# Late query and value remainders of a block-sparse attention and MoE kernel: other rows, one operation, no clearing

## Chip, cores and metric

The kernel runs on one core of a Trainium2 chip. The metric is the device time of one execution in microseconds (us). Five engines work from queues of their own, each in order: TensorE (PE, with its weight loads PEld), VectorE (DVE), ScalarE (ACT), GpSimd (POOL) and SyncE (SP), whose queue issues all the DMA transfers here.

## What is computed

Attention over 4 batches, 8 heads, 768 positions, head size 64. Each query sees its neighbours within 16 positions and 24 blocks of 32 positions, each block by its element-wise maximum of keys and its mean of values. Then a layer norm and a two-matrix feed-forward layer (512 to 2048 to 512) with a residual.

```python
k_sum = k.reshape(B, H, nb, block, D).max(axis=3)
v_sum = v.reshape(B, H, nb, block, D).mean(axis=3)
scores_l = scale * np.matmul(q, k.transpose(0, 1, 3, 2))
mask_l = np.abs(pos[:, None] - pos[None, :]) < window
scores_s = scale * np.einsum('bhsd,bhnd->bhsn', q, k_sum) + np.log(block)
scores_all = np.concatenate([np.where(mask_l, scores_l, -1e9), scores_s], axis=-1)
a = softmax(scores_all)
x = np.matmul(a, np.concatenate([v, v_sum], axis=2))     # heads side by side: [B, S, 512]
xn = (x - mean(x)) / np.sqrt(var(x) + 1e-6) * g_ln
out = x + np.maximum(xn @ w_ch1, 0.0) @ w_ch2
```

## The kernel before

The work is cut into 24 query tiles of 128 positions, each in two halves of four heads: 48 half tiles t. The first 12 (batch 0) run in float32 ("early"). The other 36 ("late") run in pairs of float16 numbers: each float32 operand is scaled by a power of two and split into its rounded value ("high") and the remainder ("low"), so that float16 matmuls give nearly float32 sums. The feed-forward layer works on 12 groups of two query tiles, again with pairs; g1 makes hidden units (h, then hh and hl), g2 adds their products into accumulators (a).

Three steps of a late half tile matter here.

- `load_q` (L601) loads the query tile twice, on rows 0 to 63 and on rows 64 to 127. ACT writes the high part to all 128 rows of qhl, then DVE overwrites rows 64 to 127 with the remainder. The key tiles hold the same 64 rows twice as well, so that one matmul contracts both parts of the query.
- `load_v` (L630) loads 128 rows of values into part 0 of vst and the tail with the block means into part 1. Part 1 holds the same data on rows 0 to 63 and on rows 64 to 127: `pv` (L787) contracts it with the high part of the last probabilities on the upper copy and with their remainder on the lower one. ACT writes the high halves of the float16 tile v16 (in the profile: v), DVE the low halves in two operations: 128 rows of part 0, and 64 rows of part 1. The low half of part 1 on rows 64 to 127 stays as `go_late` (L451) left it, zero.
- `transp` (L685) splits the probabilities and sends them through a transposing DMA to pT, which `pv` multiplies with the value tile.

Other names: raw, wf and wp are weights as loaded, decoded and split; kmax and vsum are maxima and sums of blocks; xn and xs are the normalised tile and its transposed pair; ksg, kh and kl are the keys; tx is the PE transposition of xn in the first groups; hl is the remainder of a hidden unit; spare is a filler.

No order is written by hand. A planner (class `Plan`) records every operation with an estimated cost and its dependences, and in 32 rounds of list scheduling looks for an order of all five queues; the best round is issued (`issue`, L352; hence all instructions carry line L373). Where PE would wait over 800 ns while the first weights are prepared, the planner puts fillers, small transpositions (spare, L370), in front of the wait. Two of its cost rules touch the change: a DVE operation costs its width over 0.96 plus a fixed part, and 119 ns are added where its first operand begins on row 64.

```python
fixed = {"tensor_tensor_reduce": 78, "reciprocal": 90}.get(op, 70) + 61 * pointers
fixed += 119 * (self.box(ins[0])[1] == D)
return n / (1.92 if op == "tensor_scalar" and not psum else 0.96) + fixed, 0.0
```

Of the kernel before, what the change touches and what calls it, by code (L numbers as in the profile page):

```python
# [15 lines left out]
F16 = mybir.dt.float16  # L16
U32 = mybir.dt.uint32
AF = mybir.ActivationFunctionType
ALU = mybir.AluOpType
AX = mybir.AxisListType  # L20

B, H, S, D = 4, 8, 768, 64
DM, DFF = 512, 2048
P = 128
# [38 lines left out]
    qs=("qs", "qw0"),  # L63
# [314 lines left out]
def body(ctx: ExitStack, tc, qt, qa, qe, kt, ks, va, vb, vs, g_ln, w1, w2, blocks, out):  # L378
# [5 lines left out]
    def work(tag, name, shape, dt=F32, bufs=1):  # L384
        return pl.tile(wp, shape, dt, tag, name, bufs)
# [17 lines left out]
    nc = pl  # L403
# [5 lines left out]
    late = {}  # L409
# [40 lines left out]
    @pl.step  # L450
    def go_late():  # L451
        late["p"] = prob[0], work("k0_0", "p3", [P, 4, NE])
        for x in late["p"]:
            nc.gpsimd.memset(x[:, :, NC:], 0.0)
        for i in range(2):
            t = late["v", i] = work(f"v16_{i}", f"v16_{i}", [P, 2, 4, 2, D], F16)
            nc.gpsimd.memset(t[:], 0.0)

    turn = {}

# [6 lines left out]
    def stg(tag, shape, dt=F32):  # L467
        stg_n[0] += 1
        if tag == "bst1":
            tag = ("bst", "qs")[stg_n[0] % 2]  # L470
        elif tag in ("bst", "qs"):
            tag = home(tag)
        return work(tag, f"{tag}{stg_n[0]}", shape, dt, 1 + (tag == "xn"))
# [126 lines left out]
    @pl.step  # L600
    def load_q(t):  # L601

        T, hh = divmod(t, 2)
        qs = stg('qs', [P, 4, P])
        for half in range(2):
            nc.sync.dma_start(qs[D * half : D * half + D], qt[T, hh])
        qhl = work(f"qhl{t % 2}", f"qhl{t}", [P, 4, P], F16)
        sc = bt["s", T // NT][:, 1:2]
        nc.scalar.activation(qhl[:], qs[:], AF.Copy, scale=sc)
        nc.vector.scalar_tensor_tensor(qhl[D:], qs[D:], sc[D:], qhl[D:], ALU.mult, ALU.subtract)  # L610
        st[t, "q"] = qhl

    @pl.step
# [15 lines left out]
    @pl.step  # L629
    def load_v(t):  # L630
        T, hh = divmod(t, 2)
        vt = vst[hh]
        nc.sync.dma_start(vt[:, 0], va[T, hh])
        for half in range(2):
            nc.sync.dma_start(vt[64 * half : 64 * half + 32, 1], vb[T, hh])
        w = late["v", hh]
        sv = bt["s", T // NT][:, 0:1]
        nc.scalar.activation(w[:, :, :, 0, :], vt[:], AF.Copy, scale=sv)
        for rows, i in ((P, 0), (D, 1)):
            nc.vector.scalar_tensor_tensor(  # L640
                w[:rows, i, :, 1, :], vt[:rows, i], sv[:rows], w[:rows, i, :, 0, :], ALU.mult, ALU.subtract
            )

    @pl.step
    def qk(t):
# [346 lines left out]
    def attend(t):  # L992
        if t < NEARLY:
            early_k(t)
            early_qk(t)
            for pr in range(2):
                softmax(t, pr)
            for pr in range(2):
                early_transp(t, pr)
                early_pv(t, pr)  # L1000
        else:
            load_q(t)
            for pr in range(2):
                load_k(t, pr)
            qk(t)
            for pr in range(2):
                softmax(t, pr)
            load_v(t)
            transp(t)
            pv(t)  # L1010
        if t % 2 and t < 8:
            norm(t // 2)
        if t == 3:
            spare()
# [29 lines left out]
    for t in range(NEARLY):  # L1044
        if t % 2 == 0:
            fetch_tail(t // 2)
        attend(t)
    go_late()

    for m in range(16):  # L1050
# [16 lines left out]
    for t in range(8, 2 * TT + 1):  # L1067
# [7 lines left out]
        b, i = divmod(t, 2 * NT)  # L1075
# [66 lines left out]
```

## Time and profile before

| | before |
|---|---|
| median of 3 runs | 633.12 us (632.31 to 633.8) |
| profiled execution, its own time | 633.28 us |
| its span, first to last instruction | 631.5 us |
| mean granted TensorE clock | 0.994 |
| DMA | 93.15 MB, mean 148 GB/s |

The span is what the trace covers; the execution's own time is 1.8 us longer. "Busy" of an engine is the time in which it has an instruction; PE's ends are modelled, so its pieces overlap slightly. In a timeline row the columns are start (us), duration (us), engine, line, operation and names (out<-in), shapes, count, and in brackets the idle time just before with what ended it. In a row of windows each engine has its busy time with the number of instructions; the last three columns are the granted clock, the DMA share and GB/s.

### The profile page before, as it was taken

What the parts mean: (1) busy time and instruction counts of PE and PEld (TensorE: products, weight loads), DVE (VectorE), ACT (ScalarE), POOL (GpSimd) and SP (SyncE); (2) the same over time, 40 slices, a digit from 0 to 9 for tenths busy, and PEclk for the clock granted to TensorE, in tenths of its full rate; (3) what the DMA queues carried; (4) which work ended last, traced back from release to release, by engine and by line L of the source; (5) the groups of instructions that cost most, each with busy time, mean ns of one, the idle gap of its engine ahead of it and who ended that gap; (6) DMA issues with size and microseconds to landing.
All of it is one profiled execution on the core that took longest, in us unless ns stands there. A gap on an engine that the chain in (4) does not pass through costs nothing.

```text
span 631.5 us, 13489 instructions
## 1 busy us (share of the span) xinstructions
PE 611.5 (97%) x4656; PEld 435.3 (69%) x4656; DVE 445.3 (71%) x1190; ACT 390.9 (62%) x1036; POOL 202.7 (32%) x413
## 2 busy tenths in 40 slices
PE   8988999999999999999999999999999999999997
PEld 5777766675676777667667677667766766666665
DVE  4799998999979999767956866866756844421212
ACT  4888898779988868768856674763763742110100
POOL 5221320023546536543533352533523512100000
PEclk9979999999999999999999999999999999999999
DMA  8980577626998888797855545556736513110000
GB/s 257 383 294 15 174 240 235 197 78 180 240 236 213 210 175 186 167 226 202 199 122 126 135 121 126 141 133 139 154 102 125 117 46 58 27 50 1 18 18 33
DMA packets 124997, 93.15 MB, mean 148 GB/s; under 512 B 84864, under 2 KB 107392, under 8 KB 124928
## 3 DMA queue, kind: packets, MB, share of 16 engines
q1 hardware_dynamic: 124928, 92.29, 56.1%
q8 instruction: 36, 0.59, 0.4%
q14 instruction: 33, 0.27, 0.1%
HBM read 66.27 MB, written 6.29 MB: 115 GB/s over the span
## 4 chain that ended last, share of the span: by engine, by line
PE 55%; DVE 18%; DMA 13%; ACT 4%; issue 4%; SPq 2%; POOL 2%; ACTq 0%; POOLq 0%; DVEq 0%
PE a L373 27%; PE h L373 24%; DMA ksg<-in_kt 4%; DMA raw<-in_w 3%; DMA qs<-in_qa 2%; DVE wf L373 2%; SPq L373 2%; PE o L373 2%; PE s L373 2%; DVE p L373 2%; DVE hl L373 2%; DMA bst<-in_vs 2%; DVE wp L373 2%; DVE raw L373 1%; DVE x L373 1%
## 5 line engine op out<-in xcount | busy, mean ns | idle before, releaser
L373 PE MATMUL h<-xs,wp 128*128 128x256 f16 x2304 | 272.7, 273 | 3.5 <-DVE hl L373 1.7
L373 PEld LDWEIGHTS <-wp 128*128 128x128 f16 x2304 | 223.6, 98 | 45.2 <-DVE hl L373 2.5
L373 PE MATMUL a<-wp,hh 128*128 128x512 f16 (+1 forms) x768 | 226.5, 377 | 0.0
L373 PE MATMUL a<-wp,hl 128*128 128x512 f16 x384 | 144.7, 377 | 0.0
L373 ACT ACTIVATE hh<-h 128x512 f16<-128x512 f32 x96 | 56.6, 590 | 132.1 <-PE h L373 104.3
L373 DVE SCALAR_TENSOR_TENSOR hl<-h,hh 128x512 f16<-128x512 f32 x96 | 65.6, 684 | 87.9 <-ACT hh L373 87.6
L373 PEld LDWEIGHTS <-hh 128*128 128x128 f16 x784 | 75.9, 98 | 63.2 <-issue 0.4
L373 ACT ACTIVATE p<-p,mn,sv 128x184 f32<-128x184 f32 x144 | 76.1, 530 | 19.1 <-POOL mn L373 17.9
L373 POOL TENSOR_TENSOR p<-p,p 128x512 f16<-128x512 f32 x72 | 69.4, 971 | 29.0 <-ACT p L373 26.3
L373 PEld LDWEIGHTS <-hl 128*128 128x128 f16 x392 | 38.3, 98 | 44.6
L373 DVE CUSTOM_DVE_ANT_0 p<-s,mask 128x184 f32<-128x184 f32 x144 | 43.3, 341 | 26.1 <-PE s L373 25.9
L373 ACT ACTIVATE kh<-ksg,sv 128x368 f16<-128x368 f32 x72 | 42.5, 593 | 19.2 <-POOL ksg L373 19.1
L373 POOL TENSOR_SCALAR mn<-mn,sv 128x2 f32<-128x2 f32 x72 | 31.7, 441 | 66.8 <-DVE mn L373 66.6
L373 DVE SCALAR_TENSOR_TENSOR x<-a,wsc,x 128x512 f32<-128x512 f32 (+1 forms) x48 | 35.3, 738 | 21.6 <-PE a L373 21.4
L373 DVE SCALAR_TENSOR_TENSOR kl<-ksg,sv,kh 128x368 f16<-128x368 f32 x72 | 46.1, 666 | 1.5 <-ACT kh L373 1.5
L373 POOL TENSOR_TENSOR x<-x,rc 128x256 f32<-128x256 f32 x36 | 24.9, 692 | 67.7 <-DVE x L373 63.7
L373 POOL COPY ksg<-ksum 128x48 f32<-128x48 f32 x72 | 21.5, 302 | 53.4 <-DMA ksg<-in_kt 44.0
L373 DVE SCALAR_TENSOR_TENSOR v<-vst,sv,v 128x256 f16<-128x256 f32 x72 | 38.1, 552 | 0.1
L373 ACT CAST p<-p 128x512 f16<-128x512 f32 x72 | 33.9, 504 | 0.3
L373 DVE TENSOR_REDUCE x<-o 128x256 f32<-128x512 f32 x36 | 24.5, 683 | 8.1 <-PE o L373 8.0
L373 PEld LDWEIGHTS <-pT 128*128 128x128 f16 x432 | 23.7, 98 | 7.3 <-DMA pT<-p 2.8
L373 PEld LDWEIGHTS <-qhl 128*128 128x128 f16 x288 | 24.0, 98 | 5.0
(128 smaller groups left out, 795.3 us busy)
## 6 DMA issues: line engine op xcount, KB each, us to landing
raw<-in_w SPq DMA_DIRECT2D x32, 512.0 KB
ksg<-in_kt SPq DMA_DIRECT2D x72, 184.0 KB
out_x<-x SPq DMA_DIRECT2D x23, 256.0 KB
qw<-in_qt SPq DMA_DIRECT2D x36, 128.0 KB
vst<-in_va SPq DMA_DIRECT2D x36, 128.0 KB
qs<-in_qt SPq DMA_DIRECT2D x36, 128.0 KB
vst<-in_vb SPq DMA_DIRECT2D x84, 32.0 KB
bst<-in_ks SPq DMA_DIRECT2D x12, 192.0 KB
```

The costliest lines, as they stand in the source:

```text
L373: getattr(getattr(nc, self.ops[i].engine), op)(*a, **k)
```

## The change

The query remainder goes to rows 0 to 63 instead of 64 to 127; since the key rows are there twice, the sum over both halves is the same. The value remainder is written by one DVE operation over both parts and all 128 rows. The low half of part 1 on rows 64 to 127 is then no longer zero but the remainder, which adds the product of both remainders to the result. As every element is now written, the two clearings of the value tiles on POOL go.

```diff
@@ go_late
         for i in range(2):
-            t = late["v", i] = work(f"v16_{i}", f"v16_{i}", [P, 2, 4, 2, D], F16)
-            nc.gpsimd.memset(t[:], 0.0)
+            late["v", i] = work(f"v16_{i}", f"v16_{i}", [P, 2, 4, 2, D], F16)
@@ load_q
         nc.scalar.activation(qhl[:], qs[:], AF.Copy, scale=sc)
-        nc.vector.scalar_tensor_tensor(qhl[D:], qs[D:], sc[D:], qhl[D:], ALU.mult, ALU.subtract)
+        nc.vector.scalar_tensor_tensor(qhl[:D], qs[:D], sc[:D], qhl[:D], ALU.mult, ALU.subtract)
@@ load_v
         nc.scalar.activation(w[:, :, :, 0, :], vt[:], AF.Copy, scale=sv)
-        for rows, i in ((P, 0), (D, 1)):
-            nc.vector.scalar_tensor_tensor(
-                w[:rows, i, :, 1, :], vt[:rows, i], sv[:rows], w[:rows, i, :, 0, :], ALU.mult, ALU.subtract
-            )
+        parts = [w[:, :, :, n, :].rearrange("p i j d -> p (i j) d") for n in range(2)]
+        nc.vector.scalar_tensor_tensor(
+            parts[1], vt.rearrange("p i j d -> p (i j) d"), sv, parts[0], ALU.mult, ALU.subtract
+        )
```

By the planner's rules the query operation gets cheaper by the 119 ns, and with the changed costs it finds another order for every queue. Three places follow; a minus marks a row of before only, a plus one of the change only.

On PE, around the preparation of the first weights, between the hidden unit h_306 and the hidden unit h_328 (wps is the sum that scales a weight block):

```order
 L373 MATMUL h_306<-xs_138,wp_300 128x256
-L370 MATMUL spare<-ident 128x128 x2
+L370 MATMUL spare<-ident 128x128 x3
 L373 MATMUL wps_0_317<-wacc,ones 128x8
+L370 MATMUL spare<-ident 128x128 x16
 L373 MATMUL tx_219<-ident,xn_218 128x128 x4
-L370 MATMUL spare<-ident 128x128 x11
+L370 MATMUL spare<-ident 128x128 x9
 L373 LDWEIGHTS wp_286
 L373 MATMUL h_328<-xs_192,wp_286 128x256
```

The 13 fillers of this gap become 28; with two other gaps (8 to 11 and 17 to 23) there are 69 fillers in place of 45.

On DVE, at the same time, the rows from the eviction of the transposed tile (xs_192), which h_328 reads, to the second half of the weight conversion wp_318 (wsc are the scales of a weight block, kmax block maxima). Before:

```order
L373 TENSOR_REDUCE kmax_408<-qs_413 128x12
L373 TENSOR_TENSOR xs_192<-tx_219,xs_192 128x512
L373 TENSOR_SCALAR wsc<-wsc 128x1
L373 TENSOR_SCALAR wf_344<-raw_301 128x512
L373 TENSOR_SCALAR wsc<-wsc 128x1
L373 TENSOR_SCALAR wf_345<-raw_302 128x512
L373 TENSOR_SCALAR wsc<-wsc 128x2
L373 SCALAR_TENSOR_TENSOR wf_344<-raw_301,wf_344 128x512
L373 TENSOR_REDUCE kmax_408<-bst_414 128x12
L373 SCALAR_TENSOR_TENSOR wp_318<-raw_273,wsc,wp_318 128x512
L373 SCALAR_TENSOR_TENSOR wp_318<-raw_274,wsc,wp_318 128x512
```

Now:

```order
L373 TENSOR_SCALAR wsc<-wsc 128x1
L373 TENSOR_SCALAR wf_344<-raw_301 128x512
L373 TENSOR_SCALAR wsc<-wsc 128x1
L373 TENSOR_SCALAR wf_345<-raw_302 128x512
L373 TENSOR_SCALAR wsc<-wsc 128x2
L373 SCALAR_TENSOR_TENSOR wf_344<-raw_301,wf_344 128x512
L373 TENSOR_TENSOR xs_192<-tx_219,xs_192 128x512
L373 SCALAR_TENSOR_TENSOR wp_318<-raw_273,wsc,wp_318 128x512
L373 TENSOR_REDUCE kmax_408<-qs_413 128x12
L373 TENSOR_REDUCE kmax_408<-bst_414 128x12
L373 SCALAR_TENSOR_TENSOR wp_318<-raw_274,wsc,wp_318 128x512
```

The eviction now stands behind six scaling and decoding operations that followed it, and ahead of one block maximum that preceded it; at the last row of each piece the sets ahead are equal.

On DVE, where the first late value tiles (v_0, v_1) are split. Before:

```order
L373 SCALAR_TENSOR_TENSOR v_0_263<-vst_77,sv_437,v_0_263 64x4x64
L373 SCALAR_TENSOR_TENSOR x_177<-a_4_0_406,wsc,x_177 128x512
L373 SCALAR_TENSOR_TENSOR x_123<-a_4_0_404,wsc,x_123 128x512
L373 SCALAR_TENSOR_TENSOR qhl_535<-qw_534,sv_437,qhl_535 64x512
L373 TENSOR_SCALAR rc_493<-sum_489,sv_437 128x4
L373 SCALAR_TENSOR_TENSOR v_1_264<-vst_78,sv_437,v_1_264 128x4x64
L373 SCALAR_TENSOR_TENSOR v_1_264<-vst_78,sv_437,v_1_264 64x4x64
```

Now:

```order
L373 SCALAR_TENSOR_TENSOR qhl_518<-qs_517,sv_437,qhl_518 64x512
L373 SCALAR_TENSOR_TENSOR v_1_264<-vst_78,sv_437,v_1_264 128x8x64
L373 TENSOR_REDUCE kmax_705<-qw_715 128x12
L373 SCALAR_TENSOR_TENSOR x_177<-a_4_0_406,wsc,x_177 128x512
L373 TENSOR_SCALAR rc_493<-sum_489,sv_437 128x4
L373 RECIPROCAL rc_493<-rc_493 128x4
L373 ISA p_262,mn_505<-s_0_503,mask_477 128x184
```

The value pair of v_1 has become one operation of 8 times 64 elements on 128 rows; the query operation keeps its shape, 64 rows of 512.

On POOL the two clearings, which stood on either side of the scaling of the block sums (vsum) at the start of the late stage, are gone.

## The prediction

> **What bounds the kernel now.** I read the page's first two parts, then busy times by stage, then TensorE's gaps one by one, then the chain of waits.
>
> ```profile
> PE 611.5 (97%) x4656; PEld 435.3 (69%) x4656; DVE 445.3 (71%) x1190; ACT 390.9 (62%) x1036; POOL 202.7 (32%) x413
> ...
> DVE  4799998999979999767956866866756844421212
> ```
>
> TensorE (PE) is busy for 97% of the span, so the ceiling of any edit elsewhere is small. VectorE (DVE) shows 71%, but its digits are 9 through most of the first 24 slices (380 us) and then fall away: the average mixes two regimes. The view by stages separates them (us, then busy us of PE, its weight loads, DVE, ACT, POOL):
>
> ```profile
> 50.00:75.00 25.00, 21.99 (x187) 18.95 (x186) 24.88 (x67) 21.27 (x64) 4.64 (x9) 1.00 0.24 76
> 100.00:125.00 25.00, 22.67 (x167) 16.27 (x168) 21.23 (x59) 21.26 (x64) 2.05 (x5) 1.00 0.62 201
> 143.00:280.00 137.00, 132.40 (x1076) 95.07 (x1075) 121.41 (x328) 112.56 (x296) 68.78 (x128) 1.00 0.84 202
> 300.00:600.00 300.00, 300.00 (x2287) 207.32 (x2286) 179.30 (x462) 144.72 (x346) 91.31 (x163) 1.00 0.45 102
> ```
>
> From 300 to 600 us PE never idles: what DVE saves there is worth nothing. From 143 to 280 us, where the late query tiles begin, PE idles 4.6 of 137 us while DVE is 89% busy. From 50 to 75 us DVE is full (24.88 of 25) and PE has 3 us of idle, besides fillers. So the span is PE's fixed work plus its gaps, and all gaps worth having lie before 280 us. PE's timeline lists them; the figure in brackets is the idle time and what ended it:
>
> ```profile
> 100.37 0.55 PE L373 MATMUL pp<-ident,p 128*128 128x128 f32 x3 [0.51 <-ACT p L373]
> ...
> 124.94 0.33 PE L373 MATMUL pp<-ident,p 128*128 128x128 f32 x1 [0.19 <-ACT p L373]
> ...
> 146.64 1.48 PE L373 MATMUL h<-xs,wp 128*128 128x256 f16 x12 [0.71 <-DMA xs<-x]
> ...
> 265.74 0.74 PE L373 MATMUL o<-v,pT 128*128 128x128 f16 x12 [1.27 <-DMA pT<-p]
> 279.08 1.49 PE L373 MATMUL h<-xs,wp 128*128 128x256 f16 x12 [1.53 <-DVE hl L373]
> ```
>
> The first two rows are the first and the last of five gaps between 100 and 125 us, 2.4 us in all; the others are three of six between 143 and 280 us, 4.6 us in all. None follows the last row until the work runs out.
>
> **The query remainder (36 operations).** Its width and row count stay; only the first row moves from 64 to 0. Durations alone say that this is worth nothing:
>
> ```profile
> L373 DVE SCALAR_TENSOR_TENSOR qhl<-qs,sv,qhl x18: 750/752/1104, 144.3 to 489.5; 64x512 f16<-64x512 f32 x18
> L373 DVE SCALAR_TENSOR_TENSOR wp<-raw,wsc,wp x31: 715/743/753, 44.0 to 153.8; 128x512 f16<-128x512 f32 x31
> ```
>
> The same operation of the same width from row 0 has a median of 743 ns against 752. But DVE operations overlap, and what counts is the distance from start to start:
>
> ```profile
> 59.36 2.74 DVE L373 SCALAR_TENSOR_TENSOR wp<-raw,wsc,wp 128x512 f16<-128x512 f32 x4
> 62.02 0.16 DVE L373 TENSOR_SCALAR rc<-sum 128x4 f32<-128x4 f32 x1
> ...
> 215.88 0.88 DVE L373 SCALAR_TENSOR_TENSOR v<-vst,sv,v 128x256 f16<-128x256 f32 x2
> 216.79 0.75 DVE L373 SCALAR_TENSOR_TENSOR qhl<-qw,sv,qhl 64x512 f16<-64x512 f32 x1
> 217.57 0.69 DVE L373 BATCH_NORM_STATS2 s<-x 128x6 f32<-128x512 f32 x1
> ```
>
> Four row-0 operations take 62.02 - 59.36 = 2.66 us, 0.665 each, and the next starts 0.08 us before the last ends. The query operation does not overlap: the value pair ends at 216.76 and it starts at 216.79; it ends at 217.54 and the next starts at 217.57. With the usual overlap it could have started at 216.68, so it occupies 217.57 - 216.68 = 0.89 us, and from row 0 it should occupy 0.665: **0.22 us less each**. The bounds are 0.01 (the medians) and 0.22; I take 0.22, because a 64-row operation from row 0, the second of the value pair, does overlap.
>
> [...]
>
> **The value remainder (72 operations become 36).**
>
> ```profile
> L373 DVE SCALAR_TENSOR_TENSOR v<-vst,sv,v 64x256 f16<-64x256 f32 x36 | 20.6, 572 | 0.0
> L373 DVE SCALAR_TENSOR_TENSOR v<-vst,sv,v 128x256 f16<-128x256 f32 x36 | 19.2, 533 | 0.0
> ...
> 225.51 0.79 DVE v L373 x2
> ```
>
> The last row is from the chain: the pair occupies 0.79 us. One 512-wide operation should occupy 0.665: **0.125 us less per tile**. The added rows 64 to 127 cost nothing, since the two forms of equal width differ by less than their spread (the 64-row form has the larger mean). The means, 0.55 us, lie above the 0.44 us of an undisturbed one, because some wait for POOL. Between "the wait per operation stays" and "per element stays" this is worth 0.1 us per tile or nothing; I take nothing.
>
> [...]
>
> **What of it reaches the end.** DVE saves 36 x 0.22 + 36 x 0.125 = 12.4 us in all. Before 280 us there are 16 query operations and 14 value pairs: 3.5 + 1.75 = 5.3 us. The chain says how much of them was waited for:
>
> ```profile
> 144.30 1.10 DVE qhl L373
> ...
> 221.43 0.76 DVE qhl L373
> ...
> 155.99 0.15 DVE v L373
> ...
> 242.35 0.87 DVE v L373 x2
> ```
>
> These are the first and last of five query pieces (4.2 us) and of ten value pieces (4.5 us) on the chain before 280 us. Five times 0.22 is 1.1 us, and 0.125 / 0.79 = 16% of 4.5 is 0.7 us: **1.8 us off the chain**. Bounds: nothing (another wait, such as the transposition DMA of the 1.27 us gap, ends equally late) and 4.6 us (every PE gap after 143 us closes). I take 1.8.
>
> **The dropped clearing.**
>
> ```profile
> L373 POOL MEMSET v<- 128x1024 f16 x2 | 1.9, 952 | 13.4 <-ACT wf L373 12.8 <-PE o L373 0.7
> L373 ACT ACTIVATE v<-vst,sv x36: 705/710/722, 150.3 to 532.2; 128x512 f16<-128x512 f32 x36
> ```
>
> The two clearings run at 127.8 and 129.8 us, POOL idles 13.4 us ahead of them, and the first reader of a value tile starts at 150.3 us. Twenty microseconds of other work cover them: 0 of at most 1.9 us. If the cover were gone, it would be the scaling of the block sums between them that gains.
>
> **The new order.** The planner's costs changed, so every queue is reordered from about 45 us on, before any edited instruction runs. Two places matter. First, TensorE gets 69 fillers instead of 45. Second, the eviction of the transposed tile that hidden unit h_328 waits for (xs_192) stands behind six more operations and one reduction fewer:
>
> ```profile
> 70.59 0.54 DVE L373 TENSOR_REDUCE kmax<-qs 128x12 f32<-128x384 f32 x1
> 71.05 0.68 DVE L373 TENSOR_TENSOR xs<-tx,xs 128x512 f16<-128x512 f32 x1
> 71.64 0.14 DVE L373 TENSOR_SCALAR wsc<-wsc 128x1 uint32<-128x1 uint32 x1
> ...
> 73.22 0.55 DVE L373 TENSOR_REDUCE kmax<-bst 128x12 f32<-128x384 f32 x1
> ```
>
> What stood between 71.64 and 73.22 (six operations, 1.58 us) is now ahead, the reduction (71.05 - 70.59 = 0.46 us) behind: PE starts that group **1.1 us later**. Its gap is filled anyway:
>
> ```profile
> 69.84 1.36 PE L370 MATMUL spare<-ident 128*128 128x128 f32 x11
> ...
> 71.78 5.29 PE L373 MATMUL h<-xs,wp 128*128 128x256 f16 x47 [0.47 <-DVE wsc L373]
> ```
>
> Eleven fillers take 1.36 us, of which the last one's modelled end is some 0.27: 0.109 us each, so 24 more are 2.6 us. By the weight conversion two microseconds on (wp_318), DVE has done the same set of operations in both orders, so DVE itself is not late; only PE is, by 1.1 us, and the 2.4 us of gaps between 100 and 125 us end with DVE, ACT and DMA events that PE's lateness leaves where they are. I cost it at 0; bounds 0 and +2.6 us.
>
> Sum against the profiled execution (633.28 us: a span of 631.5 and 1.8 around it): 633.28 - 1.8 = 631.5. That execution lies 0.16 us above the median shown, so I say **631.4 us**.
>
> **The rivals.**
> - Relief hidden: two of the three late gaps quoted end with a DMA, and the loads on SP's queue stay. A shorter DVE then only waits longer, and reordered queues open as many small gaps as they close: 633.1, within 1.2 either way. Against: DVE is 89% busy there.
> - More than the chain shows: the orders also let all gaps after 143 us close: 633.1 - 4.6 = 628.5. Against: each gap has another releaser.
> - Slower: the later start at 71 us and the 24 fillers are not recovered. Place: the gap ahead of h_328; price: up to 2.6 us; it decides if the five gaps from 100 to 125 us fail to shrink by as much as PE starts later. 633.1 + 2.6 = 635.7. For it: more fillers stand exactly where the planner leaves PE waiting.
> - The query operation does not get shorter, held for another reason than its first row: only the value term is left, 633.1 - 0.7 = 632.4.
>
> **How the numbers follow.** Chances: forecast 0.36 (630.2 to 632.6), hidden 0.28, more 0.11, slower 0.20, not shorter 0.05. A measurement of this kernel can tell about 0.2%, 1.3 us, from no change, so faster is below 631.8 and slower above 634.4. Three quarters of the forecast (0.27), all of "more" and a little of "hidden" (0.06) are faster: 0.44. Nearly all of the slower case and a little of hidden (0.03) are slower: 0.22. The rest, 0.34, is same. The range leaves out the lower half of "more" and the end of the slower case: 629.0 to 635.7.
>
> **What would show it.** Right: the query operation's start-to-start distance is 0.66 to 0.68 us and overlaps its neighbours; 36 value operations of about 0.74 us; DVE busy near 432; PE's gaps after 143 us sum to some 2.8 us, those from 100 to 125 us to about 1.3; the bulk of h_328 starts near 72.9. Wrong: a distance still near 0.8; gaps after 143 us of 4 us or more; PE gaps that reappear after 300 us; or the gap sum before 125 us grows by the fillers' 2.6 us.

## The result and the profile after

| | before | after |
|---|---|---|
| median of 19 runs each, beside each other | 633.60 us (632.22 to 637.13) | 637.85 us (634.62 to 640.60) |
| ratio, with its 95% interval | | 1.0059 [1.0041, 1.0077] |
| mean granted clock, mean over the runs that list it | 0.994 (17 runs of the next comparison) | 0.990 |

The change is slower, outside the forecast range (629.0 to 635.7). A second comparison of the unaltered change, told below, gave 1.0047 [1.0023, 1.0071]. The profiled execution of after is its fastest (634.62 us, span 632.8), so it shows the change at its best; a more usual execution comes further down.

The page's first part, after:

```profile
PE 612.6 (97%) x4680; PEld 437.4 (69%) x4680; DVE 433.6 (69%) x1154; ACT 392.3 (62%) x1036; POOL 207.2 (33%) x411
```

DVE's busy time fell by 11.7 us (445.3 to 433.6), almost the 12.4 us of the sum. The two edited operations, DVE's timeline of after (start, duration, names):

```profile
267.77 0.59 DVE L373 SCALAR_TENSOR_TENSOR kl<-ksg,sv,kh 128x368 f16<-128x368 f32 x1
268.28 0.74 DVE L373 SCALAR_TENSOR_TENSOR qhl<-qw,sv,qhl 64x512 f16<-64x512 f32 x1
268.94 0.73 DVE L373 SCALAR_TENSOR_TENSOR x<-a,wsc,x 128x512 f32<-128x512 f32 x1
...
272.56 0.72 DVE L373 SCALAR_TENSOR_TENSOR v<-vst,sv,v 128x512 f16<-128x512 f32 x1
273.22 0.67 DVE L373 SCALAR_TENSOR_TENSOR hl<-h,hh 128x512 f16<-128x512 f32 x1
```

From row 0 the query operation begins 0.08 us before its predecessor ends (268.36 against 268.28) and takes 268.94 - 268.28 = 0.66 us to the next start; the value operation takes 273.22 - 272.56 = 0.66. Both are the forecast 0.665 us. So these operations do what was said; the loss must come from elsewhere. Windows of after, with the columns as in the prediction:

```profile
100.00:125.00 25.00, 22.77 (x171) 16.82 (x170) 24.09 (x68) 21.25 (x65) 2.58 (x5) 1.00 0.79 254
...
143.00:280.00 137.00, 136.87 (x1115) 99.25 (x1113) 120.74 (x326) 116.01 (x305) 73.81 (x132) 1.00 0.89 211
280.00:300.00 20.00, 17.38 (x142) 12.09 (x141) 10.93 (x24) 15.11 (x42) 5.84 (x10) 1.00 0.75 188
```

From 143 to 280 us TensorE now idles 0.13 us in place of 4.6: more relief than forecast. But from 280 to 300 us it idles 2.6 us, in one piece, where before shows no idle time:

```profile
280.00:300.00 20.00, 20.00 (x163) 14.15 (x161) 14.21 (x38) 15.71 (x43) 7.62 (x14) 1.00 0.78 212
```

TensorE's timeline of after there, and SyncE's queue of DMA issues (SPq) just before:

```profile
288.79 1.47 PE L373 MATMUL h<-xs,wp 128*128 128x256 f16 x12 [2.62 <-DMA xs<-x]
```

```profile
283.37 0.34 SPq L373 DMA_DIRECT2D qw<-in_vs  x1
283.81 1.40 SPq L373 DMA_DIRECT2D qs<-in_qt  x2
285.31 1.28 SPq L373 DMA_TRANSPOSE xs<-x  x1
```

TensorE waits for the transposed tile xs, the first operand of a new group. DVE has finished that tile at 283.06; its transposing DMA is issued at 285.31, behind a load of value blocks (in_vs) for the next batch's sums and two loads of queries.

**A usual execution.** A second and a third profile were taken of the unaltered change. The second (633.33 us) is again the fastest of its runs; the third (638.48 us, span 636.7) is near the median and shows what the first two do not. Two of its windows, and TensorE's longer gaps in them:

```profile
100.00:125.00 25.00, 22.92 (x160) 16.29 (x159) 20.52 (x54) 18.82 (x57) 2.43 (x5) 0.93 0.73 224
...
280.00:300.00 20.00, 17.71 (x118) 11.68 (x116) 11.88 (x30) 15.36 (x42) 5.96 (x12) 0.91 0.82 218
```

```profile
105.89 0.38 PE L373 MATMUL wps<-wacc,ones 128*128 128x4 f32 x2 [1.18 <-ACT wf L373]
106.87 0.49 PE L373 MATMUL o<-vst,pT 128*128 128x128 f32 x2 [0.59 <-ACT pT L373]
...
291.06 2.20 PE L373 MATMUL h<-xs,wp 128*128 128x256 f16 x12 [2.29 <-DVE kl L373]
```

The gap at 288 to 291 us is there again. The view names DVE's kl as what ended it here, not the transposition; DVE came late to kl because a block sum just before it had waited for its load:

```profile
289.14 0.68 DVE L373 TENSOR_REDUCE vsum<-qw 96x16 f32<-96x512 f32 x1 [2.09 <-DMA qw<-in_vs]
```

Behind the gap the granted clock is 0.91 over the 20 us: the 12 matmuls after it take 2.20 us where they took 1.47 in the first profile. The same happened at 106 us (0.93 over 25 us). By estimate these two drops cost 25 x 0.07 + 20 x 0.09 = 3.5 us. In the comparison with 17 runs of before and 12 of the change beside each other, span times (1 - clock), averaged over the runs, is 3.9 us for before and 6.0 for after. By this estimate, **2.1 of the 3.1 us between the mean spans are clock.** It counts every stretch with a lower clock, the start too, where TensorE may have been waiting anyway.

How far TensorE has come with its useful work, each matmul of the trace counted by its columns at the distance of an undisturbed stream (0.107 us for 256 float16 columns) and fillers left out, in us of work; up to 1 us can be matmuls missing from a trace:

| | by 143 us | by 280 us | by 300 us |
|---|---|---|---|
| before | 122.1 | 251.3 | 271.2 |
| after, first two profiles | 119.6, 119.8 | 253.6, 254.2 | 270.8, 271.6 |
| after, usual execution | 118.2 | 250.8 | 266.8 |

The changed kernel is 2.3 to 3.9 us behind at 143 us, more than makes it up by 280 us in the first two profiles, and loses that again within the next 20 us. So the gap by itself does not explain the loss: with it, these two executions end within 1.3 us of before's profile (spans of 632.8 and 631.6 against 631.5). The third is 5.2 us longer; by 280 us it is 0.5 us behind, and from there to 300 us it does 16.0 us of work where before does 19.9.

### The profile page after: what moved, and what is told of

It is laid out like the page before. It is cut to its first block, busy times and chain, and to the rows that moved or that the text cites. A ratio compares the mean times of both kernels' runs of the same rounds, so it can differ in the third digit from the quotient of the medians.

```text
span 632.8 us, 13472 instructions
## 1 busy us (share of the span) xinstructions
PE 612.6 (97%) x4680; PEld 437.4 (69%) x4680; DVE 433.6 (69%) x1154; ACT 392.3 (62%) x1036; POOL 207.2 (33%) x411
## 4 chain that ended last, share of the span: by engine, by line
PE 69%; DVE 9%; DMA 9%; ACT 6%; issue 3%; SPq 2%; POOL 1%; ACTq 0%; DVEq 0%; POOLq 0%
PE a L373 31%; PE h L373 29%; PE s L373 3%; PE o L373 3%; ACT p L373 2%; DVE wf L373 2%; SPq L373 2%; DVE raw L373 2%; DMA qs<-in_qa 1%; PE v L373 1%; DMA ksg<-in_kt 1%; DMA qw<-in_qa 1%; DMA vw<-in_va 1%; DVE hl L373 1%; DMA bst<-in_ks 1%
## 5 line engine op out<-in xcount | busy, mean ns | idle before, releaser
L373 PE MATMUL h<-xs,wp 128*128 128x256 f16 x2304 | 271.6, 273 | 3.1 <-DMA xs<-x 2.6
L373 POOL TENSOR_SCALAR mn<-mn,sv 128x2 f32<-128x2 f32 x72 | 33.7, 470 | 55.3 <-DVE mn L373 54.8
L373 POOL TENSOR_TENSOR x<-x,rc 128x256 f32<-128x256 f32 x36 | 29.3, 815 | 66.3 <-DVE x L373 64.9
L373 DVE SCALAR_TENSOR_TENSOR kl<-ksg,sv,kh 128x368 f16<-128x368 f32 x72 | 44.3, 641 | 2.0 <-ACT kh L373 1.0
L373 DVE SCALAR_TENSOR_TENSOR v<-vst,sv,v 128x512 f16<-128x512 f32 x36 | 28.8, 801 | 2.3 <-ACT v L373 2.3
L373 ACT ACTIVATION_READ_ACCUMULATOR p<-p,mn,sv 128x1 f32 x144 | 27.4, 190 | 0.0
```

The lines of the kernel that those rows point to most:

```text
L373: getattr(getattr(nc, self.ops[i].engine), op)(*a, **k)
```

## Experiments

Every kernel was run beside before on the same chip; in the five comparisons the median of before was 633.7 to 634.3 us. The theories' names are those of the quoted expectations.

### Order or operations

The first kernel plans with before's operations and then issues the new ones in their places.

```diff
             nc.gpsimd.memset(t[:], 0.0)
+            pl.ops[-1].calls = []
...
+        pl.ops[-1].calls = [("scalar_tensor_tensor", (qhl[:D], qs[:D], sc[:D], qhl[:D], ALU.mult, ALU.subtract), {})]
...
+            pl.ops[-1].calls = []
+            if i == 0:
+                pl.ops[-1].calls = [("scalar_tensor_tensor", whole, {})]
```

> The changed operations in the order of before (the planner is shown the old operations, and the new ones are issued in their places; the second value operation and the clearings are left out). Theory ORDER (the loss of 4 us is the new order's): 0 to 2 us faster than before, since the order is the old one and DVE saves some 12 us of which 1.8 are on the chain. Rival OPERATIONS (one longer value operation holds POOL, or makes something late): slower than before by 2 us or more. Rival CLOCK (the loss is a lower granted clock that follows the early order): as ORDER for the time, with a clock as in before.

Measured: 642.25 us, ratio 1.0117 [1.0086, 1.0149], the slowest of the first four. Its DVE and PE timelines:

```profile
281.98 0.75 DVE L373 SCALAR_TENSOR_TENSOR v<-vst,sv,v 128x512 f16<-128x512 f32 x1 [5.47 <-DMA vst<-in_vb]
```

```profile
286.50 2.74 PE L373 MATMUL h<-xs,wp 128*128 128x256 f16 x12 [5.50 <-DVE hl L373]
```

The merged value operation waits 5.47 us for a load of tail rows, with h behind it. This shows a dependence that the prediction overlooked. Before, DVE read only rows 0 to 63 of part 1. So the load of rows 64 to 95 for the next tile but one, which uses the same buffer, needed to wait for ACT alone, and in the order of before 20 of these loads stand ahead of the place where the merged operation was put. It reads those rows now, and so waited for that load (and took its remainder there from that later tile). The kernel does not answer whether the order or the operations cost the time; a later one repairs it.

The second kernel is the opposite: the plan of the change, with before's operations issued (clearings beside the scaling of the block sums).

> The operations of before (query remainder on rows 64 to 127, two value operations, clearings) in the order of the change. ORDER: slower than before by 4 us or more, and slower than the change by 0 to 2 us. OPERATIONS: as before, within 1.5 us.

Measured: 639.66 us, 1.0089 [1.0065, 1.0113]; the unaltered change beside it:

> The change, unaltered, for another profile of it beside the others. All theories: 4 us above before. ORDER expects the difference in the gaps of TensorE before 150 us; CLOCK expects it in stretches with a clock below 1.00 before 60 us, with equal gaps.

636.46 us, 1.0047 [1.0023, 1.0071]. The operations of before alone, put into the new order, lose 5.9 us (639.66 against 633.75): **the order has a price of its own.** In that same order the new operations are 3.2 us faster than the old ones, so in the order planned for them they look like a gain, though the intervals just overlap; that order with them is still slower than before. The profile with the old operations has only 1.43 us of idle near 290 us, with a clock of 1.00, and is 2.4 us behind before by 280 us already: the long gap is not the only way in which this order loses.

### Fewer fillers

43 fillers in place of 69, at the same places.

```diff
+        keep, group, seen = (6, 8, 17, 2, 0, 9), -1, 0
...
+                if seen > keep[group]:
+                    continue
```

> The change with 43 fillers in place of 69 (per gap 8, 17, 2, 0, 9 in place of 11, 23, 3, 16, 9), nothing else altered. If the added fillers push TensorE's work back (the slower rival of the prediction): 1 to 2.6 us faster than the change. If they only fill waits: as the change within 1 us. CLOCK: as the change or slower, since a TensorE that idles longer is granted less.

Measured: 640.27 us, 1.0102 [1.0078, 1.0127], slower than with all 69. Its windows:

```profile
50.00:75.00 25.00, 20.90 (x169) 18.37 (x168) 23.17 (x66) 19.46 (x60) 2.85 (x7) 0.91 0.22 67
100.00:125.00 25.00, 23.23 (x156) 16.32 (x155) 23.02 (x65) 21.45 (x66) 4.27 (x8) 0.93 0.74 250
280.00:300.00 20.00, 16.20 (x100) 10.21 (x98) 11.83 (x32) 13.11 (x36) 5.84 (x14) 0.85 0.88 193
```

TensorE does not get on sooner without them, it idles, and the clock falls to 0.91 from 50 to 75 us, where the other profiles with that early order and its 69 fillers had 1.00 (in after with TensorE busy for 23.04 us of the 25). The added fillers are not the price that the slower rival took them for.

### Each edit alone, with an order of its own

> Only the query remainder moves to rows 0 to 63; the value remainder keeps two operations and the clearings stay; the planner makes its own order for it. Theory DRAW (what decides is which waits the new order happens to leave after 143 us, not which operation changed): the time lies anywhere from 632 to 641 us and follows from this run's own gaps and clock: 628 to 630 us of span times clock, plus its gaps over 0.5 us beyond those of before. Theory MERGE (the merged value operation is at fault): 632 to 633.5 us, as before or a little faster. Theory QUERY (the query operation on rows 0 to 63 is at fault): 636 to 638 us.

> Only the value remainder becomes one operation and loses its clearings; the query remainder stays on rows 64 to 127; the planner makes its own order for it. Theory DRAW: anywhere from 632 to 641 us, and the gaps and the clock of the run account for it. Theory MERGE: 636 to 638 us. Theory QUERY: 632 to 633.5 us.

Query alone: 635.37 us, 1.0015 [0.9980, 1.0051]. Value alone: 636.39 us, 1.0042 [1.0011, 1.0074]. The value edit is nearer to the change, but the intervals overlap. Each order has large gaps of its own; PE's largest after 143 us, of query alone and then of value alone:

```profile
290.95 1.62 PE L373 MATMUL h<-xs,wp 128*128 128x256 f16 x12 [2.66 <-DMA xs<-x]
```

```profile
189.94 1.57 PE L373 MATMUL h<-xs,wp 128*128 128x256 f16 x12 [2.71 <-DVE hl L373]
...
288.80 1.48 PE L373 MATMUL h<-xs,wp 128*128 128x256 f16 x12 [2.30 <-DVE mn L373]
```

MERGE has the value run right and the query run 2 us too low, QUERY has neither; long gaps in other places are what DRAW expects, though a theory of one guilty operation is not excluded by two runs. Query alone and the change, planned apart, both have a long gap near 290 us that a transposition of xs ends.

### The query edit alone in the order of before

```diff
         nc.vector.scalar_tensor_tensor(qhl[D:], qs[D:], sc[D:], qhl[D:], ALU.mult, ALU.subtract)
+        pl.ops[-1].calls = [("scalar_tensor_tensor", (qhl[:D], qs[:D], sc[:D], qhl[:D], ALU.mult, ALU.subtract), {})]
```

> Before with its own order, instruction for instruction; only the query remainder is issued on rows 0 to 63. It isolates what the shorter VectorE occupation is worth when nothing is reordered and no dependence is added that the order does not already respect. By the prediction's sum: 0.22 us at each of the five query pieces of the chain before 280 us, so 1.1 us less than before, about 632.6 us. Theory HIDDEN (the loads on SyncE's queue and the clock set the end, not VectorE): within 0.2% of before, 632.4 to 635 us, with query operations 0.665 us apart all the same.

Measured: 633.41 against 633.84 us, 0.9994 [0.9979, 1.0010]: 0.4 us faster, anything from 1.3 faster to 0.6 slower. HIDDEN fits, but the interval does not exclude the 1.1 us of the prediction's sum. In its trace the last PE gap after 143 us has grown from 1.53 to 2.58 us while DVE has more time to spare:

```profile
278.58 1.48 PE L373 MATMUL h<-xs,wp 128*128 128x256 f16 x12 [2.58 <-DVE hl L373]
```

### Both edits in the order of before, loads behind

The order is given by a table: that of before, with the 20 loads right behind the merged operations. The same edit, with other tables, makes all the joined orders below.

```diff
-        for _, i in sorted([*zip(best[1], range(len(after))), *((t, -1) for t in fills)]):
+        raw = zlib.decompress(base64.b85decode("".join(TABLE)))
+        for i in struct.unpack(f"<{len(raw) // 2}h", raw):
```

> All of the change's operations in the order of before; the merged value operation stands where the first of the pair stood, and the 20 loads of rows 64 to 95 of a tail (the upper copy for the next tile but one) that stood ahead of it in SyncE's queue follow right behind it, since it reads those rows now. In the earlier kernel with the old order these loads stayed ahead, so that the merged operation read and waited for the next tile's rows. Theory DEPENDENCE (what the merging costs is that these loads, and all behind them in SyncE's queue, must wait for VectorE): 636 us or more, and gaps after 143 us of 6 us or more, against 4.4 in before. Otherwise, if that dependence is free and the order of before is simply the better one: 631 to 633.5 us, gaps after 143 us of 4.4 us or less.

Measured: 635.89 us, 1.0018 [0.9996, 1.0040], gaps after 143 us 4.9 us in the profile. Neither branch of the expectation: five runs of twelve have spans of 630.6 to 631.4 us, seven of 633.9 to 635.4, and what parts them is open. With the dependence respected, both edits cost 1 to 2 us in the order of before (the interval reaches from -0.3 to 2.5), against 2.7 to 4.3 in their own order (the intervals overlap with that of its second comparison); the added dependence is at most a part of it.

### Halves of the order

Both kernels take their order from tables that join the two orders at about 143 us.

> The changed kernel's operations, in the order of before up to about 143 us (45 fillers, no edited operation has run by then) and in the order of the change from there on. In the traces TensorE has done 122.4 us of useful work by 143 us in before and 118.6 to 120.1 in the three profiles of the change. Theory EARLY (the new order before 143 us costs 2.3 to 3.8 us and that is what makes the change slower): 122 us of work by 143 us, and 630.5 to 633.5 us in all, as the part behind 143 us gains 1 to 2 us. Theory LATE (the stage from 260 to 300 us, where loads fill SyncE's queue, costs it): 635 to 637.5 us, still with one gap over 2.3 us near 288 us and a granted clock below 0.95 behind it in usual executions.

> The mirror image: before's operations, in the order of the change up to about 143 us (69 fillers) and in the order of before from there on. EARLY: 118.5 to 120 us of useful work by 143 us, and 635.5 to 637.5 us in all. LATE: 633 to 634.5 us, the lag being taken up by the gaps that end with loads. If both E2 and E3 lie between, each part has its share and the two ratios add up to that of the change, 1.006.

Old order first, with the change's operations: 636.28 us, 1.0045 [1.0019, 1.0072]. New order first, with before's operations: 642.49 us, 1.0141 [1.0109, 1.0172]. The first gives LATE its number: with all of before's fillers and 121.5 us of work by 143 us it is as slow as the change. Its joint costs nothing that the count shows: by 280 us it has 254.1 us of work done, as much as the change's first two profiles. Its long gap and its windows row behind it:

```profile
289.24 2.72 PE L443 MATMUL h<-xs,wp 128*128 128x256 f16 x12 [4.17 <-DMA xs<-x]
```

```profile
280.00:300.00 20.00, 15.83 (x98) 9.89 (x97) 10.63 (x23) 14.42 (x41) 5.55 (x10) 0.91 0.74 186
```

TensorE was 2 us further by 143 us than in the change (119.6 to 119.8), and the wait for the same tile is 1.6 us longer. The second contradicts both theories: halves that fit into other wholes do not add up. It has a gap of its own just behind the joint,

```profile
156.23 2.74 PE L444 MATMUL h<-xs,wp 128*128 128x256 f16 x12 [3.59 <-DMA xs<-x]
```

so a part of its 8.7 us is the joint's. A third joint, the change's order up to about 205 us and before's (loads behind) from there:

> The changed kernel's operations in the order of the change up to about 205 us and in the order of before (loads behind the merged operation as in the run with the whole order of before) from there on. If the order from 260 to 300 us decides: two gaps of 1 to 2 us at 265 and 279 us in place of the long one at 288, and 634 to 636 us as with the whole order of before. If what was lost before 143 us decides: 636.5 to 639 us.

637.93 us, 1.0068 [1.0042, 1.0094], with 2.06 us of idle right behind the joint, and 1.43 ahead of 283.58 us:

```profile
210.66 7.07 PE L443 MATMUL h<-xs,wp 128*128 128x256 f16 x48 [2.06 <-DVE qhl L443]
```

The clock falls behind the first of these gaps: the 48 matmuls take 7.07 us, where such a row takes 5.42 undisturbed. The kernel does not restore the time of before; its joint costs too much to say more.

### What holds the transposition: sums, loads, or queue

First the arithmetic of four chunks of the next batch's sums is left out, then their loads as well (the last lines of the diff, and the same for the query chunks).

```diff
+        if b == 3 and c < 2:
+            pl.ops[-1].calls = [("memset", (t[:, c * 16 : c * 16 + 16], 0.0), {})]
...
+        if b == 3 and c >= 4:
+            pl.ops[-1].calls = []
...
         nc.sync.dma_start(vv[:], vs[b, c])
+        if b == 3 and c < 2:
+            pl.ops[-1].calls = []
```

> The changed kernel with its order and all its loads; only the arithmetic of four chunks of the next batch's block statistics is left out (batch 3: absolute sums of query chunks 4 and 5 on ScalarE, sums and absolute sums of value chunks 0 and 1; the two value sums on VectorE become clearings that wait for no load). In the two profiles of the change these are the operations that stand in ScalarE's and VectorE's queues waiting 3.0 and 2.7 us for loads ahead of the work that the gap of 2.6 us at 288 us waits for. Theory PLACE (the loss is this one gap and the clock that falls behind it): the gap falls below 0.5 us, no other gap over 1 us takes its place after 143 us, the mean granted clock over the runs rises from 0.990 to 0.994, and the time is 631 to 634 us. Theory ELSEWHERE (that gap is only what the two profiles happened to show; the loss of 3 to 4 us is made up of other places): 635 to 637 us with the clock at 0.990, whether or not the gap closes.

> As the run that left out four chunks of the next batch's statistics, but their four loads are left out too (query chunks 4 and 5, 256 KB each; value chunks 0 and 1, 192 KB each). With the sums alone gone the gap stayed (3.4 us), VectorE and ScalarE were idle for 5 us ahead of it, the transposition was ready to go at 278.1 us and SyncE's queue came to it at 283.6 us, with the DMA engines 84 to 110% busy. Theory LOADS (SyncE's in-order queue and the DMA engines behind it are what binds from 260 to 290 us, not VectorE): the gap falls below 1 us, the clock stays at 1.00 there, 631 to 634 us. Rival: the gap stays over 2 us, bound by something else, 636 to 638 us.

Without the sums: 638.13 us, 1.0063 [1.0031, 1.0094], nothing gained. Without the loads too: 633.06 us, 0.9979 [0.9963, 0.9996]. **In the changed kernel the four loads, 0.9 MB, are worth about 5 us; their arithmetic alone is worth nothing.** Some of this is what any kernel paced by its loads would gain: at the 211 GB/s of the change's window from 143 to 280 us, 0.9 MB are 4.3 us, by estimate. No run leaves the same loads out of before, so it is not shown that they are what sets the two kernels apart. The first of the two, DVE, then SP's queue, then PE and the windows:

```profile
277.43 0.69 DVE L373 TENSOR_TENSOR x<-xn,x 128x512 f16<-128x512 f32 x1
```

```profile
280.60 0.84 SPq L373 DMA_DIRECT2D ksg<-in_kt  x2
281.49 0.43 SPq L373 DMA_DIRECT2D qw<-in_vs  x1
282.37 1.14 SPq L373 DMA_DIRECT2D qs<-in_qt  x2
283.61 1.52 SPq L373 DMA_TRANSPOSE xs<-x  x1
```

```profile
287.64 2.72 PE L373 MATMUL h<-xs,wp 128*128 128x256 f16 x12 [3.42 <-DMA xs<-x]
```

```profile
280.00:300.00 20.00, 16.58 (x103) 10.27 (x102) 8.96 (x20) 9.65 (x26) 5.48 (x10) 0.83 0.67 183
```

DVE has the tile ready at 277.43 + 0.69 = 278.12, where the profile of after had it at 283.06. SP comes to it at 283.61, after another transposition and loads that it issues one after the other. Meanwhile DVE idles for 7.0 us behind ACT, ACT for 4.4 behind POOL, and POOL for 6.3 for a load of keys. What DVE and ACT were spared became 5.5 us of waiting for SP's queue. The second kernel, over the same 20 us:

```profile
280.00:300.00 20.00, 19.94 (x160) 13.88 (x159) 12.77 (x32) 14.65 (x39) 7.28 (x13) 1.00 0.71 188
```

No gap, and the clock stays at 1.00. (In that profile TensorE came 2.6 us later to 143 us than in the first, so a part of the missing gap is that it arrives later; the medians, of 10 and 12 runs, don't depend on it.)

Then the transposition was moved ahead of four loads, and the split of the hidden unit h_38 ahead of two sums, with all work done:

> The changed kernel; in its order only the neighbourhood of the long gap is altered: the transposing DMA of the tile that PE waits for at 288 us goes out as soon as its tile is split, ahead of four loads (one key load, one chunk of value sums, the query tile in two halves) that stood ahead of it, and the split of the hidden unit h_38 goes ahead of two block sums on VectorE and of a key split on ScalarE. All work is done. Theory PLACE: the transposition is issued about 1.5 us earlier, the gap falls from 2.5 to 3.4 us to below 1.5 us, the drop of the clock behind it goes, 633 to 635 us. Theory LOADS in its strict form (what is moved back there becomes late instead): another gap of 1 us or more opens within 20 us behind it, 636 to 638 us.

637.40 us, 1.0053 [1.0029, 1.0078]. SP and PE:

```profile
283.16 1.24 SPq L443 DMA_TRANSPOSE xs<-x  x1
284.44 0.61 SPq L443 DMA_DIRECT2D ksg<-in_kt  x1
```

```profile
292.83 2.78 PE L443 MATMUL h<-xs,wp 128*128 128x256 f16 x24 [2.14 <-DVE hl L443]
```

The transposition is issued ahead of the four loads, and the 12 matmuls that waited for it now run without a gap, at 286.61 us. But a gap of 2.14 us opens soon behind them, after 12 more matmuls of h, ended by hl; DVE comes late to hl, as a block sum ahead of it waits 2.28 us for its load (in_vs). PLACE falls, LOADS in its strict form holds: what is sent earlier makes the next thing late. The two waits, for SP's queue and for that load on DVE, run beside each other, and this run and the one without the sums each removed only one.

Last, the same four loads from ScalarE's queue in place of SyncE's, and then all 44 loads for sums of batches 2 and 3, on the change and on before:

```diff
-                getattr(getattr(nc, self.ops[i].engine), op)(*a, **k)
+                getattr(getattr(nc, getattr(self.ops[i], "via", self.ops[i].engine)), op)(*a, **k)
...
+        if b == 3 and c < 2:
+            pl.ops[-1].via = "scalar"
```

> The changed kernel with all its work; the four loads that the run before left out are issued from ScalarE's queue, at the same places of the order, instead of SyncE's. [...] Theory QUEUE (what binds is that SyncE issues one transfer after the other and holds the transposition behind these loads): as without the loads, gap near 288 us under 1.5 us, 633 to 635 us. Theory ENGINES (the DMA engines themselves, over 84% busy there, are the bound): the gap stays above 2 us, 636 to 638 us.

> The changed kernel; all 44 loads for the statistics of batches 2 and 3 go out from ScalarE's queue. QUEUE: 630 to 634 us, if ScalarE has room for 44 issues of about 0.4 us (18 us; it is 81 to 87% busy from 143 to 300 us, so it may not); with ScalarE as the new bound 637 to 642 us. ENGINES: 636 to 638 us.

> Before, with the same 44 loads from ScalarE's queue. It shows whether the relief of SyncE's queue, if there is any, is one of the change or one that before could have as well. QUEUE: 630 to 633 us. ScalarE the new bound: 636 to 641 us. ENGINES: 633 to 635 us.

Four loads: 640.53 us, 1.0099 [1.0070, 1.0129]. ACT's timeline (ACTq is its queue of DMA issues) and PE's:

```profile
273.65 0.39 ACTq L373 DMA_DIRECT2D bst<-in_qa  x1
...
282.27 0.63 ACT L373 ACTIVATE bst<-bst 128x512 f32<-128x512 f32 x1 [4.38 <-DMA bst<-in_qa]
```

```profile
293.70 2.72 PE L373 MATMUL h<-xs,wp 128*128 128x256 f16 x12 [4.51 <-DMA xs<-x]
```

QUEUE's forecast fails, but the kernel does not decide between the two theories, because ACT pays a new price. The load goes out at 273.65 and its reader starts at 282.27, 8.6 us later; ACT works in order and stands still for 4.38 us of that, with all its other work behind it. So the tile is ready only at 289.14 (283.06 in after). SP's queue then holds it for 0.55 us (289.14 to 289.69), where in after it held it for 2.25: that part of the wait did go, and what ACT lost hides what it was worth. This trace shows no faster transfer from ACT's queue, though the 8.6 us are one load's; which DMA engines carried it, no view here shows.

44 loads: 655.08 us, 1.0323 [1.0276, 1.0370], and on before 647.81, 1.0214 [1.0172, 1.0257]. Both have a gap of 15 to 16 us early on, as large as most of the loss of the first (20.7 us) and all of the second's (13.5). There ACT's work stands behind the first of these loads in ACT's queue, which is issued only after a wait; on the change:

```profile
42.54 0.90 PE L373 MATMUL pp<-ident,p 128*128 128x128 f32 x3 [15.14 <-ACT pT L373]
```

They say nothing of the late stage. No kernel that does all the work was measurably faster than before.

### The third profile

> The change unaltered, a third profile. The two profiles so far were among its fastest executions (634.6 and 633.3 us against medians of 637.9 and 636.5). Theory PLACE: a usual execution of 636 to 638 us shows the gap at 288 us at 3 us or more and a granted clock under 0.95 in the 20 us from it. Theory ELSEWHERE: the gap stays 2.6 us with the clock at 1.00 there, and the missing 3 us are found in another stretch.

Told above: the gap stayed near 2.3 us and the clock fell to 0.91 behind it, so the first half of PLACE's condition fails and the second holds; a second drop at 100 to 125 us was in neither theory.

## Why the prediction was wrong

- **Right: the operations.** 0.66 us from start to start for both, DVE 11.7 us less. (The clearing was not tried by itself.) In before all 36 query operations, on row 64, start 0.03 us after the end of the operation ahead of them; in after, on row 0, 35 start 0.07 to 0.09 us ahead of that end, and the one at 278.69 us found DVE idle. Why they were kept apart on row 64, no run shows. The waits for POOL that the prediction names are in before's trace: eight value operations of 64 rows that started while POOL's x (x<-x,rc) ran took 0.82 to 0.83 us and ended 0.27 to 0.28 us after it; the shortest value operation took 0.44. POOL's x takes longer in after: 1.05 us where it starts 0.16 to 0.17 us into a merged value operation (at 342.68 us, for one), against 0.78 us so far into the first of a pair (at 341.41 us in before).
- **Did not reach the end: "1.8 us off the chain".** TensorE's gaps from 143 to 280 us did close, beyond the forecast (4.6 to 0.13 us), but in the first two profiles what they gave back was lost in one wait of 2.5 to 2.6 us at 288 us. For the query edit alone, in an unchanged order, the sum had 1.1 us; measured were 0.4 [-0.6 to 1.3], which excludes neither 1.1 nor nothing. The rival "relief hidden" named the reason, that the late gaps end with transfers; I held DVE's 89% against it, and passed over the DMA share in the same row, 0.84, and SP's queue.
- **Wrong: "the new order, I cost it at 0".** This is the step that failed, and it decided the sign. The order alone, with before's operations in it, measured 5.9 us slower than before; with the new operations it was 2.7 to 4.3. The late start at 71 us was forecast (+1.1 us) and was there: h_328 starts at 74.39 us in the profile of after, whose startup is 1.5 us longer. The five gaps from 100 to 125 us were to absorb it and did not: TensorE's idle in that window is 2.23 us (25 - 22.77) against 2.33 before, and by 143 us it is 2.5 us behind (1.5 of this is the startup; the second profile, without it, is 2.3 behind). That was made good by 280 us, in the third profile nearly; what was not is the loss from 280 to 300 us. The slower rival had the sign and nearly the size (635.7), but at the wrong place: with before's order and fillers up to 143 us the time is the same 636.3, and with fewer fillers it is worse.
- **Left out: the clock.** The prediction sums gaps and takes 1.00 for granted. Over the profiles of all the kernels here, behind 143 us: after single gaps of up to 1.79 us the clock stayed at 1.00; of ten gaps of 2.06 to 2.71 us, five were followed by slow matmuls (2.06, 2.19, 2.29, 2.66, 2.71) and five were not (2.14, 2.30, 2.51, 2.58, 2.62); after all seven of 3.42 to 5.50 us it fell. Shorter gaps close together can do it too: it fell behind 1.60 and 0.86 us within 2 us, and at 106 us in the third profile behind 1.18 and 0.59. The change's own three profiles had 2.51 and 2.62 (1.00 from 280 to 300 us) and 2.29 (0.91). So gaps that sum to less than before's can cost more than before's. What parts the five gaps of 2.06 to 2.71 us behind which it fell from the other five is not shown.
- **Left out: a dependence.** "The added rows 64 to 127 cost nothing" is right for the operation's duration, and overlooked that reading them ties 20 loads to VectorE. The first experiment shows the wait (5.47 us) where the order ignores it; where it is respected, both edits together cost 1 to 2 us in the order of before.

The cause, as far as it is shown: the new order costs more than the operations gain. Where the change loses against before's profile is the stretch from 280 to 300 us. From 260 to 290 us the DMA engines are busy for 0.90 of the time (0.78 in before), and TensorE waits there in one long piece, for a transposition that SP's queue issues late or for DVE held by a load. In the first two profiles it had come there 2 to 3 us further on and lost only that; in the third it had not, and the clock fell too. Without four of the loads the change is as fast as before.

Not settled: that these loads, and not something else in the order, make the difference, since before was not run without them; how the 3 to 4 us divide between the drop at 106 us, in half of the profiles with the change's early order (5 of 10; none of 5 with the order of before there), the drop at 290 us, and the gaps; what parts the two groups of runs of both edits in the old order. Before and most of the kernels have one profile each, so how often a gap and its drop occur is not known. No other order was faster than that of before; why it suits these loads better is not explained.

## What to carry to other kernels

Before counting an engine's saving, look in the same window at the DMA share and at the queue that issues transfers: where those set the pace, faster compute may only arrive early and wait (here TensorE's gaps from 143 to 280 us closed, and it waited 2.6 us at 288 us, with a DMA share of 0.90 from 260 to 290 us). Count idle time of TensorE by its longest pieces, not by its sum, since one long wait can cost as much again in clock as it lasts (a gap of 3.42 us was followed by 0.83 over 20 us, by estimate 3.4 us). When an edit makes an operation read more rows, list who writes those rows next: a merged operation can tie transfers to an engine that they did not wait for before (here 20 loads to VectorE).

## Not expected of the hardware

- A load of 256 KB issued from ScalarE while SyncE's loads were running had its reader start 8.6 us after the issue; a load of the same tile issued from SyncE in the profile of before, 3.6 us (273.02 to 276.59 us). It is one load of each.
- Taking 26 dummy transpositions out made the kernel 3.8 us slower (640.27 against 636.46 us): the clock fell to 0.91 between 50 and 75 us.
